# The first forward stage of a spectral mixing kernel: float32 products in place of a split pair

## The chip, the cores and the metric

The kernel runs on one core of a Trainium2 chip. The metric is device time in microseconds (us) for one run of the whole program. A core has engines that run side by side, each with its own queue of instructions taken strictly in the order in which the program lists them: PE (TensorE, matrix products; the loading of weights is shown apart as PEld), DVE (VectorE), ACT (ScalarE), POOL (GpSimd) and SP (SyncE, which here only starts transfers). POOL and ACT start a few transfers too. An engine waits for another by a semaphore.

## The reference

The input x has 2048 rows (s) and 512 columns (d). Two branches are computed from it and mixed by a gate of each row:

```
g = sigmoid(sum over d of x * gate_w)                 one number per row
a = irfft2( rfft2(x) * (w_r + i w_i) )                over rows and columns
b = gelu(x @ w1 + b1) @ w2 + b2                       w1 512 x 1792, w2 1792 x 512
out = g * a + (1 - g) * b
```

All of it is float32. rfft2 keeps 257 of the 512 column frequencies.

## The kernel before, in words

The Fourier transforms are done as matrix products with tables of cosines and sines, and the dense branch as plain matrix products. To reach float32 precision at the fast rate of PE, each operand is split into two parts of type float32r: a high part h, which ACT makes by a copy that rounds, and a low part l = value - h, which DVE makes by a subtraction. A product of two split operands is three PE products: h with h, h with l, l with h.

The rows are cut into 16 groups j of 128 rows. The forward stage is `forward(j)`, called once for each j in the order `NORD` (0, 4, 8, 12, 1, 5, ...):

- The columns of x are folded by symmetry. `eo` holds sums and differences of column blocks (L696, two DVE steps), `w` sums and differences of those (L699, two DVE steps). So `w` has four blocks of 128x128, by s (sum or difference) and c (cosine or sine).
- `w` is split into `eoh` (ACT, L704) and `eol` (DVE, L706). For j = 0 this is done in two halves, for the others in one step of 512 columns.
- The first stage multiplies them on PE with the column table `cf`, which was split when the program was built. `high` is four products, of 258 or 254 columns, of h with the table's high and low parts. `low` is four products of 130 columns, of l with the table's high part. They collect in the PSUM tile `pd`. The frequencies 0, 64, 128 and 192 have table entries that are exact without a low part, by scaling factors that a later table takes out again; this saves their low columns. The table is 2 x 128 x 576 elements.
- `pd` holds the high parts' sums and the low columns' sums in different places. ACT copies the first to the high part of `zb` (L745, two steps). DVE forms the low part of `zb` by a subtraction (L747, two steps), and adds the low columns' sums to it (L751, two steps). `zb` is the split input of the second stage. L754 reduces the gate's columns, which ride along in the table as extra columns written by L617 and L618 (high and low part), to the gate's logit.
- The second stage multiplies `zb` with the row table `tf` of this j (`py`, six products of 258 columns), and the results go to the big tile y.

Beside this the dense branch runs for four blocks c of 512 rows, in two halves of 7 of the 14 blocks f of w1 and w2: `ph` is x @ w1 for one block, gelu by ACT in PSUM (L1127), the split into `g` (L551, L552), and `po` is the product with w2. Each `ph` is 12 products of 512 columns, each `po` three for each f. The x of the dense branch is split into `mxh` and `mxl` (L642 to L647, L674 to L678), the weights into `wa..h`, `wa..l`, `wb..h`, `wb..l` (L1061 to L1069). Some weights' low parts are made by ACT (the negative of h) and a transfer of POOL that adds the original to it (L495).

After the forward stage follow, mostly on DVE, radix-4 steps and the filter, then for each c the inverse: `pz` (L987 and after) and `pa` products on PE, `od` (ACT), `u`, `v` and `w` (DVE, L1023 to L1033). For two of the four c the result is joined to the dense branch by an adding transfer of POOL (`w<-ba`) and stored (`out<-w`); for the last c the parts are joined on DVE (`o`, L1168 to L1209) and stored.

The order of all work is laid down when the program is built. Each step is entered in a graph with its engine, an assumed cost, the tiles that it reads and writes, and a rank. A list `RANKS` at the head of the file gives each step's rank; `schedule` then plays the graph through with the assumed costs, always taking the lowest rank that is ready, and the instructions are emitted in the order that comes out. All engines and the transfer queues are ordered in this way. PE's first instructions are 14 products of zeros (`none`) that warm it up.

Of the kernel before, what the change touches and what calls it, by code (L numbers as in the profile page):

```python
# [11 lines left out]
F32 = mybir.dt.float32  # L12
# [5 lines left out]
P = 128  # L18
# [3 lines left out]
HD = D // 2  # L22
# [4 lines left out]
TE, TW = 320, 576  # L27


EXACT = [0, 64, 128, 192]  # L30
NX = len(EXACT)
FORD = np.concatenate([np.arange(1, HD, 2), EXACT, [f for f in range(0, HD, 2) if f not in EXACT], [HD]])
# [23 lines left out]
def _tables():  # L56
# [3 lines left out]
    def cs(c, f):  # L60

        th = 2 * np.pi * np.asarray(f)[None, :] * d / D
        v = -np.sin(th) if c else np.cos(th)
        n = np.array([0.5 if g in (64, 192) else 1.0 for g in f])
        e = np.where(np.abs(v) > 0.6, np.where(n == 0.5, BIG, 1.0), SMALL) * np.sign(v)
        return np.where(np.isin(f, [*EXACT, HD])[None, :], e, v)

    BIG, SMALL = 2276 / 4096, 942.75 / 4096
    factor = np.ones(D)
    factor[128] = np.sqrt(2.0)  # L70
    factor[[64, 192]] = BIG * np.cos(np.pi / 8) + SMALL * np.sin(np.pi / 8)

    cf = np.zeros((2, P, TW), np.float32)
    even = FORD[P + NX:HD]
    for c in range(2):
        h, l = _split(cs(c, FORD[:P]))
        cf[c][:, :P], cf[c][:, P:2 * P] = l, h
        h, l = _split(cs(c, [*EXACT[c:], *even, *([HD] if c else [])]))
        cf[c][:, TE + 2:TE + 2 + P] = h
        cf[c][:, TE + 2 + P:TE + 2 + 2 * P - NX] = l[:, NX - c:P - c]  # L80
        assert not np.delete(l, np.arange(NX - c, P - c), 1).any()
# [8 lines left out]
    ]) / factor[f]  # L90
# [344 lines left out]
def tile_kernel(ctx: ExitStack, tc: tile.TileContext, xt, xc, w1, w2, b1, b2, x0g, wf, wrev, out, consts):  # L435
# [40 lines left out]

    def c_pe(n, k=1):
        return k * (n / 2400 + 0.0135) + 0.005

    def v(emit, n, reads, writes, rank=BULK, more=0.0):  # L480
        return add("vec", c_vec(n) + more, 0.12, emit, reads, writes, rank)

# [31 lines left out]

    gw, gs, gg = (one(n, [P, 2, 2], parts=2) for n in ("gw", "gs", "gg"))

    cft = buf("ctab", [P, 2, TW], F32R, "cf", parts=4)

    def cf_of(*cs):
        return [(cft, k) for c in cs for k in (c, 2 + c)]  # L520
# [802 lines left out]
```

## Time and profile before

| what | value |
| --- | --- |
| median of three runs | 372.4 us (372.05 to 372.67) |
| profiled execution, span from the first to the last instruction | 370.0 us |
| profiled execution's own time beside the span | not recorded apart; the runs' median is 2.4 us above the span |
| PE busy | 365.0 us, 1845 products |
| DVE busy | 337.1 us, 748 instructions |
| ACT busy | 224.2 us, 415 instructions |
| POOL busy | 34.0 us |
| moved by transfers | 61.20 MB, 165 GB/s on average |

The page gives busy time and share of the span for each engine, then the chain of work that ended last: followed backwards from the last instruction, at each step to what released it or to the instruction before it on its engine. A group's row gives line, engine, operation, output tile and input tiles, shapes, count, then busy time and the mean of one in ns, then the engine's idle time in front and what ended it. In a row of waits stand who waited, for whom, the total, the number of times and the longest. A row of a stage table has the stretch, its length, then busy us and count for PE, PEld, DVE, ACT and POOL, the granted clock of PE, the DMA share and GB/s; for one tile only the engines that touch it are listed. A line can be that of a helper: all products have L504, so they are told apart by their tiles. A PE product's listed length is longer than its distance to the next, because products are pipelined.

### The profile page before, as it was taken

How to read it: one execution, taken by the hardware profiler on the slowest of the kernel's cores; microseconds unless marked ns; L12 is line 12 of the kernel's file. 1: busy time of each engine (PE TensorE's matmuls, PEld its weight loads, DVE VectorE, ACT ScalarE, POOL GpSimd, SP SyncE). 2: the span in 40 equal slices, each digit the busy share in tenths (PEclk: the TensorE clock that was granted, in tenths of full speed). 3: DMA queues.
4: the chain of work that ended last, by engine and by line, in shares of the span. 5: the costliest groups of instructions: out<-in, count | busy, mean ns of one | idle time of the engine just before them, and what ended most of it. 6: DMA issues, size and time to landing. Idle time of an engine off the chain costs nothing.

```text
span 370.0 us, 5589 instructions
## 1 busy us (share of the span) xinstructions
PE 365.0 (99%) x1845; PEld 311.2 (84%) x1845; DVE 337.1 (91%) x748; ACT 224.2 (61%) x415; POOL 34.0 (9%) x54
## 2 busy tenths in 40 slices
PE   8999999999999999999999999999999999999996
PEld 7988888888888888888888888888888888888885
DVE  5999999999999999999989896789688999999993
ACT  5999676678724453555298349753955698653410
POOL 0133000000000000003033010000010000101110
PEclk9999999999999999999999999999999999999999
DMA  8999766195764582586769873216431053276456
GB/s 249 362 267 233 199 201 200 44 271 197 234 222 141 206 288 82 207 217 124 194 161 198 236 167 58 43 37 235 62 51 29 2 204 123 94 177 164 98 155 183
DMA packets 42053, 61.20 MB, mean 165 GB/s; under 512 B 4672, under 2 KB 22528, under 8 KB 41248
## 3 DMA queue, kind: packets, MB, share of 16 engines
q1 hardware_dynamic: 36120, 50.55, 41.5%
q0 software_dynamic: 5472, 9.96, 17.1%
q10 hardware_dynamic: 432, 0.33, 0.3%
q8 instruction: 14, 0.23, 0.2%
q14 instruction: 15, 0.12, 0.2%
HBM read 41.82 MB, written 16.92 MB: 159 GB/s over the span
## 4 chain that ended last, share of the span: by engine, by line
PE 97%; DMA 1%; SPq 1%; ACT 0%; issue 0%; DVE 0%; DVEq 0%
PE ph L504 41%; PE po L504 41%; PE pz L504 4%; PE pd L504 4%; PE py L504 3%; PE pa L504 3%; DMA war<-in_w 1%; PE po_23256r L504 0%; PE po_230r L504 0%; SPq L590 0%; SPq L1060 0%; ACT wa1h L1065 0%; SPq L594 0%; DVE o L1202 0%; PE pown L504 0%
## 5 line engine op out<-in xcount | busy, mean ns | idle before, releaser
L1127 ACT ACTIVATE ph<-ph,b1t 128x512 f32<-128x512 f32 x56 | 36.9, 658 | 51.0 <-PE ph L504 51.0
L963 ACT ACTIVATE sw<-y,al 64x512 f32<-64x512 f32 x32 | 22.9, 721 | 4.6 <-DVE y L826 2.1
L922 DVE TENSOR_TENSOR m<-y,wf 128x514 f32<-128x514 f32 x32 | 20.9, 688 | 0.1
L970 DVE SCALAR_TENSOR_TENSOR pq<-y,al,sw 128x256 f32<-128x256 f32 x32 | 14.6, 480 | 2.9 <-ACT sw L966 2.7
L504 PE MATMUL py<-zb,tf 128*128 128x258 f32 x96 | 16.7, 286 | 0.0
L504 PEld LDWEIGHTS py<-zb,tf 128*128 128x128 f32 x96 | 14.5, 190 | 1.2
L1177 ACT ACTIVATE o<-po,b2t 128x512 f32<-128x512 f32 x8 | 5.4, 688 | 16.6 <-PE po L504 16.5
L778 ACT ACTIVATE y<-pys 64x257 f32<-64x257 f32 x32 | 13.2, 417 | 3.3 <-DVE pys L775 2.6
L495 POOL DMA_DIRECT2D w<-ba x8 | 7.0, 899 | 77.8 <-ACT zb L990 46.2
L504 PEld LDWEIGHTS pa<-zb,ci 128*128 128x128 f32 x96 | 13.1, 190 | 1.0
L504 PE MATMUL pa<-zb,ci 128*128 128x256 f32 x96 | 13.4, 282 | 0.0
L699 DVE TENSOR_TENSOR w<-eo 128x256 f32<-128x256 f32 x32 | 13.0, 418 | 0.1
L696 DVE TENSOR_TENSOR eo<-xf 128x256 f32<-128x256 f32 x32 | 12.9, 416 | 0.0
L704 ACT ACTIVATE eoh<-w 128x512 fp32r<-128x512 f32 (+1 forms) x17 | 10.3, 606 | 4.3 <-DVE w L699 4.3
L495 POOL DMA_DIRECT2D bacc<-o x8 | 7.0, 873 | 63.6 <-ACT o L1181 50.5
L747 DVE TENSOR_TENSOR zb<-pd,zb 128x256 fp32r<-128x256 f32 x32 | 12.5, 417 | 0.3 <-ACT zb L745 0.3
L751 DVE TENSOR_TENSOR zb<-zb,pd 128x256 fp32r<-128x256 f32 (+1 forms) x32 | 12.3, 411 | 0.4
L745 ACT ACTIVATE zb<-pd 128x256 fp32r<-128x256 f32 x32 | 11.1, 384 | 1.6 <-PE pd L504 1.0
L495 POOL DMA_DIRECT2D wa7l<-in_w x1 | 0.9, 872 | 121.3 <-DVE g_1l L552 121.3
L706 DVE TENSOR_TENSOR eol<-w,eoh 128x512 fp32r<-128x512 f32 (+1 forms) x17 | 11.1, 652 | 0.3 <-PE pd L504 0.2
L991 DVE TENSOR_TENSOR zb<-pz,zb 128x512 fp32r<-128x512 f32 x16 | 10.9, 683 | 0.4 <-ACT zb L990 0.3
L990 ACT ACTIVATE zb<-pz 128x512 fp32r<-128x512 f32 x16 | 9.5, 594 | 2.7 <-PE pz L504 2.3
(596 smaller groups left out, 1297.5 us busy)
## 6 DMA issues: line engine op xcount, KB each, us to landing
wf<-in_wf SPq DMA_DIRECT2D x16, 257.0 KB, 3.5
bacc<-o SPq DMA_DIRECT2D x16, 256.0 KB, 2.8
xf<-in_xt SPq DMA_DIRECT2D x14, 256.0 KB, 4.2
wbr<-in_w SPq DMA_DIRECT2D x14, 256.0 KB, 3.6
war<-in_w SPq DMA_DIRECT2D x13, 256.0 KB, 3.9
xm<-in_xc SPq DMA_DIRECT2D x12, 256.0 KB, 4.0
tf<-tf SPq DMA_DIRECT2D x16, 192.0 KB, 3.4
bb<-bacc SPq DMA_DIRECT2D x8, 256.0 KB, 3.7
```

Of the source, the lines that this page charges most:

```text
L495: return add("pool", 2.3 * kb / 340, 3.4, lambda: nc.gpsimd.dma_start(dst(), src(), accum_op=ALU.add), reads, writes, rank)
L504: pe.matmul(ps, w, x, start=start, stop=stop)
L696: v(lambda s=s, op=op: vec.tensor_tensor(eo.ap()[:, s], x.ap()[:, 0:2], x.ap()[:, 2:4], op=op), 256, [x], [(eo, s)], feed)
L699: v(lambda s=s, op=op: vec.tensor_tensor(w.ap()[:, s], eo.ap()[:, :, 0], eo.ap()[:, :, 1], op=op), 256, [eo], [(w, s)], feed)
L706: v(lambda k=k: vec.tensor_tensor(l.ap()[:, k], w.ap()[:, k], h.ap()[:, k], op=ALU.subtract), 256 * len(ps), sub[0] + sub[1], sub[2], feed)
L747: v(lambda c=c: vec.tensor_tensor(segs(xl, c, 0, P + c), segs(ps, c, P, P + 4), segs(xh, c, 0, P + c), op=ALU.subtract), 256, [(ps, c), xh ...
L751: v(lambda o=o, i=i: vec.tensor_tensor(xl.ap()[:, :, o], xl.ap()[:, :, o], ps.ap()[:, :, i], op=ALU.add), 256, [ps], [xl], 0)
L778: a(lambda o=o, i=i: act.activation(Y[j].ap()[o:o + HP, 1], pys.ap()[i:i + HP, 1], AF.Copy), 257, [(pys, 1)], [(Y[j], 1 + k)], 0, more=0.1)
L922: v(lambda mk=mk, k=k, y=y, w=w: vec.tensor_tensor(mk.ap(), y.ap(), w.ap()[:, k:k + 1, :ND].to_broadcast([P, 2, ND]), op=ALU.mult), 514, [ ...
L963: a(lambda sw=sw, y=y, o=o, i=i: act.activation(sw.ap()[o:o + HP], y.ap()[i:i + HP, ::-1, :HD], AF.Copy, scale=al.ap()[i:i + HP, 0:1]), 51 ...
L970: v(lambda sw=sw, pq_=pq_, y=y, j=j, k=k, op=op: vec.scalar_tensor_tensor(pq_.ap()[:, k], y.ap()[:, k, :HD], al.ap()[:, 1 + j:2 + j], sw.a ...
L1127: a(lambda f=f, ps=ps: act.activation(ps.ap(), ps.ap(), AF.Gelu_apprx_tanh, bias=b1t.ap()[:, f:f + 1]), 600, [b1t], [ps], 0.9 if half else ...
```

## The change

The split of `w` goes. `w` itself, in float32, is multiplied with one float32 table. The four products of each j have 129 columns each; the two values of s no longer add up in the same columns of `pd` but stand in separate halves of it, since the fold by s already separates odd and even frequencies, so each product starts and stops its own sum. The table is 2 x 128 x 258 elements and has no low part; the exact frequencies with their factors are gone, in the table of the inverse as well, and the frequencies' order with them. The gate's columns need no low part. The two additions (L751) go. The tile `w` moves from the pool t2k (7 places) to the pool e2 (4 places), where `eoh` and `eol` were. The planner's assumed cost of the new products is written in `c_pe4`. All other functions are unchanged, but `RANKS` is a new list with a rank for each of the 1808 remaining steps, so the order of instructions on every engine is another one throughout.

```diff
-TE, TW = 320, 576
-EXACT = [0, 64, 128, 192]
-NX = len(EXACT)
-FORD = np.concatenate([np.arange(1, HD, 2), EXACT, [f for f in range(0, HD, 2) if f not in EXACT], [HD]])
+HW = P + 1
+FORD = np.concatenate([np.arange(1, HD, 2), np.arange(0, HD, 2), [HD]])
...
-    cf = np.zeros((2, P, TW), np.float32)
...
+    cf = np.zeros((2, P, 2 * HW), np.float32)
     for c in range(2):
...
+        cf[c][:, :P] = cs(c, FORD[:P])
+        cf[c][:, HW + 1:] = cs(c, FORD[P + c:HD + c])
...
-    ]) / factor[f]
+    ])
...
+    def c_pe4(n, k=1):
+        return k * (4 * n / 2400 + 0.027) + 0.005
...
-    cft = buf("ctab", [P, 2, TW], F32R, "cf", parts=4)
+    cft = buf("ctab", [P, 2, 2 * HW], F32, "cf", parts=4)
...
-        dma(lambda c=c: raw(cft.ap()[:, c], cf_d[c]), 288, [], [(cft, k) for k in (c, 2 + c)], 0.6)
+        dma(lambda c=c: sp.dma_start(cft.ap()[:, c], cf_d[c]), 129, [], [(cft, k) for k in (c, 2 + c)], 0.6)
...
-    gcol = [lambda k=k: cft.ap()[:, :, 2 * P + k:TE + k + 1:TE - 2 * P] for k in range(2)]
-    tiny(lambda: vec.tensor_copy(gcol[0](), gg.ap()), [gg], [(cft, 2), (cft, 3)])
-    tiny(lambda: vec.tensor_tensor(gcol[1](), gg.ap(), gcol[0](), op=ALU.subtract), [gg], [(cft, 2), (cft, 3)])
+    tiny(lambda: vec.tensor_copy(cft.ap()[:, :, P:P + 2], gg.ap()), [gg], [(cft, 2), (cft, 3)])
...
-        w = buf("t2k", [P, 2, 2, P], F32, f"w{j}", parts=2)
-        h, l = (buf("e2", [P, 2, 2, P], F32R, f"eo{k}{j}", parts=2) for k in "hl")
+        w = buf("e2", [P, 2, 2, P], F32, f"w{j}", parts=2)
...
-            a(lambda k=k: act.activation(h.ap()[:, k], w.ap()[:, k], AF.Copy), 256 * len(ps), sub[0], sub[1],
-              feed)
-            v(lambda k=k: vec.tensor_tensor(l.ap()[:, k], w.ap()[:, k], h.ap()[:, k], op=ALU.subtract),
-              256 * len(ps), sub[0] + sub[1], sub[2], feed)
...
-            m(high, NE, 4, [h, cft], [ps], 0)
-        m(low, 236, 4, [l, cft], [ps], 0)
+        def fold(s, cs):
+            for c in cs:
+                o = slice(HW, 2 * HW) if s == c else slice(0, HW)
+                mm(ps.ap()[:, c, o], w.ap()[:, s, c], cft.ap()[:, c, o], True, True)
+
+        for s in range(2):
+            if first:
+                for c in range(2):
+                    add("pe", c_pe4(HW), 0.25, lambda s=s, c=c: fold(s, (c,)), [(w, s), *cf_of(c)], [(ps, c)], 0)
+            else:
+                add("pe", c_pe4(HW, 2), 0.25, lambda s=s: fold(s, (0, 1)), [(w, s), cft], [ps], 0)
...
-        for o, i in ((slice(0, P), slice(0, P)), (slice(P + NX, 2 * P), slice(3 * P + NX, 4 * P))):
-            v(lambda o=o, i=i: vec.tensor_tensor(xl.ap()[:, :, o], xl.ap()[:, :, o], ps.ap()[:, :, i], op=ALU.add), 256, [ps],
-              [xl], 0)
...
 RANKS = """
...
```

More of the change, by code (lines that the diff above doesn't have):

```diff
@@ L62, in cs @@
         th = 2 * np.pi * np.asarray(f)[None, :] * d / D
[L63 to L71, printed above, removed]
-    cf = np.zeros((2, P, TW), np.float32)
-    even = FORD[P + NX:HD]
-    for c in range(2):
[L76 to L81, printed above, removed]
+        return -np.sin(th) if c else np.cos(th)
+    cf = np.zeros((2, P, 2 * HW), np.float32)
+    for c in range(2):
+        cf[c][:, :P] = cs(c, FORD[:P])
+        cf[c][:, HW + 1:] = cs(c, FORD[P + c:HD + c])
     f = FORD[:HD, None]
@@ L700, in forward @@
               [(w, s)], feed)
-        for k in (0, 1) if first else (slice(0, 2),):
-            ps = [k] if first else [0, 1]
-            sub = [[(b, p) for p in ps] for b in (w, h, l)]
-            a(lambda k=k: act.activation(h.ap()[:, k], w.ap()[:, k], AF.Copy), 256 * len(ps), sub[0], sub[1],
-              feed)
-            v(lambda k=k: vec.tensor_tensor(l.ap()[:, k], w.ap()[:, k], h.ap()[:, k], op=ALU.subtract),
-              256 * len(ps), sub[0] + sub[1], sub[2], feed)
         if j % 4 == 0:
@@ L714, in forward @@
         ps = buf("pf", [P, 2, 512], F32, f"pd{j}", parts=2, pool=pq)
-        odd, even = (slice(0, 2 * P + 2), slice(0, 2 * P + 2)), (slice(2 * P + 2, 4 * P), slice(TE, TE + 4 * P - 2 * P - 2))
-        odd_l, even_l = (slice(P, 2 * P + 2),) * 2, (slice(2 * P + 2, 3 * P + 4), slice(TE, TE + P + 2))
-        def high(ss=(0, 1), cs=(0, 1)):
-            for s in ss:
-                for c in cs:
-                    o, i = odd if s != c else even
-                    mm(ps.ap()[:, c, o], h.ap()[:, s, c], cft.ap()[:, c, i], s == 0, False)
-        def low():
-            for c in range(2):
-                for s in range(2):
-                    o, i = odd_l if s != c else even_l
-                    mm(ps.ap()[:, c, o], l.ap()[:, s, c], cft.ap()[:, c, i], False, s == 1)
-        if first:
-            for s in range(2):
+        def fold(s, cs):
[4 more added lines that the diff above has]
+            if first:
                 for c in range(2):
-                    m(lambda s=s, c=c: high((s,), (c,)), NE, 1, [(h, s), *cf_of(c)], [(ps, c)], 0)
-        else:
-            m(high, NE, 4, [h, cft], [ps], 0)
-        m(low, 236, 4, [l, cft], [ps], 0)
+                    add("pe", c_pe4(HW), 0.25, lambda s=s, c=c: fold(s, (c,)), [(w, s), *cf_of(c)], [(ps, c)], 0)
+            else:
+                add("pe", c_pe4(HW, 2), 0.25, lambda s=s: fold(s, (0, 1)), [(w, s), cft], [ps], 0)
         xh, xl = pair()
@@ L744, in forward @@
         for c in range(2):
-            a(lambda c=c: act.activation(segs(xh, c, 0, P + c), segs(ps, c, P, P + 4), AF.Copy), 256, [(ps, c)], [(xh, c)], 0)
+            a(lambda c=c: act.activation(segs(xh, c, 0, P + c), segs(ps, c, 0, P + 2), AF.Copy), 256, [(ps, c)], [(xh, c)], 0)
         for c in range(2):
-            v(lambda c=c: vec.tensor_tensor(segs(xl, c, 0, P + c), segs(ps, c, P, P + 4), segs(xh, c, 0, P + c), op=ALU.subtract),
+            v(lambda c=c: vec.tensor_tensor(segs(xl, c, 0, P + c), segs(ps, c, 0, P + 2), segs(xh, c, 0, P + c), op=ALU.subtract),
               256, [(ps, c), xh], [(xl, c)], 0)
-        for o, i in ((slice(0, P), slice(0, P)), (slice(P + NX, 2 * P), slice(3 * P + NX, 4 * P))):
-            v(lambda o=o, i=i: vec.tensor_tensor(xl.ap()[:, :, o], xl.ap()[:, :, o], ps.ap()[:, :, i], op=ALU.add), 256, [ps],
-              [xl], 0)
         n = j % 4 * 4 + j // 4
-        v(lambda: vec.tensor_reduce(logit.ap()[:, n:n + 1], ps.ap()[:, :, 2 * P:2 * P + 4], axis=mybir.AxisListType.XY, op=ALU.add),
+        v(lambda: vec.tensor_reduce(logit.ap()[:, n:n + 1], ps.ap()[:, :, P:P + 2], axis=mybir.AxisListType.XY, op=ALU.add),
           30, [ps, xl], [(logit, n)], 0)
```

147 rows, old and new, of the table RANKS are left out of this document.

## The prediction, made before the result was known

> **What bounds the kernel now.** I read the page's head and busy shares first, then the chain of waits by line, then who waited for whom on PE, then a table of busy time by stage. The first two say which engine sets the end.
>
> ```profile
> span 370.0 us, 5589 instructions
> ...
> PE 365.0 (99%) x1845; PEld 311.2 (84%) x1845; DVE 337.1 (91%) x748; ACT 224.2 (61%) x415; POOL 34.0 (9%) x54
> ...
> PE 97%; DMA 1%; SPq 1%; ACT 0%; issue 0%; DVE 0%; DVEq 0%
> ```
> ```profile
> by line: PE ph L504 41.4%; PE po L504 41.0%; PE pz L504 3.8%; PE pd L504 3.8%; PE py L504 3.2%; PE pa L504 3.1%; DMA war<-in_w 1.0%; PE po_23256r L504 0.3%; PE po_230r L504 0.3%; SPq L590 0.2%; SPq L1060 0.2%; ACT wa1h L1065 0.2%; SPq L594
> ```
> ```profile
> PE none L504 <- DVE own L796: 1.1, 1, 1.1
> PE ph L504 <- ACT wa1h L1065: 0.5, 1, 0.5
> ```
> ```profile
> 0.00:5.28 5.28, 4.23 (x14) 3.65 (x15) 1.65 (x7) 2.53 (x5) 0.65 (x16) 1.00 0.65 187
> 5.28:13.45 8.17, 7.65 (x63) 7.44 (x62) 7.66 (x23) 5.93 (x12) 0.00 (x0) 1.00 1.03 344
> 13.45:100.00 86.55, 86.55 (x484) 75.45 (x484) 82.57 (x218) 69.60 (x153) 7.19 (x8) 1.00 0.74 214
> ```
>
> 97% of the chain is PE, and PE waits for only one thing that is named after its warm-up: 0.5 us for a weight tile, near the start. The stage table (stretch, its length, busy PE, PEld, DVE, ACT, POOL with counts, granted clock, DMA share, GB/s) shows PE filled completely in the forward stage, 86.55 of 86.55 us, at full clock. DVE is busy there for 82.57 us, but the chain holds it at 0%. So a change is paid or earned on PE; time taken from DVE and ACT is worth only the gaps of PE that it closes.
>
> **What one PE instruction costs.** PE's own durations overlap, so I take the distance between starts. These rows are from the chain in order of time (start, length, what) and from the timeline.
>
> ```profile
> 12.66 0.95 PE pd L504 x8
> 19.62 0.72 PE py L504 x6
> 48.32 0.92 PE pd L504 x8
> 110.95 10.93 PE ph L504 x48
> ```
> ```profile
> 5.49 1.04 PE L504 MATMUL ph<-mxh,wa0h 128*128 128x128 f32 x8
> 6.37 0.69 PE L504 MATMUL ph<-mxl,wa0h 128*128 128x256 f32 x4
> 6.89 0.63 ACT L1065 ACTIVATE wa1h<-war 128x512 fp32r<-128x512 f32 x1 [1.49 <-DMA war<-in_w]
> 7.58 0.74 PE L504 MATMUL ph<-mxh,wa1h 128*128 128x256 f32 x4 [0.52 <-ACT wa1h L1065]
> ```
>
> 512 columns take 10.93/48 = 0.2277 us; the 258 columns of py take 0.72/6 = 0.120; 128 columns take (6.37 - 5.49)/8 = 0.110. Four times fewer columns than 512 save only half: below about 250 columns something that does not shrink with the columns, the change of weights most likely, paces PE. The old first stage sits on that floor: 3.8% of 370.0 us is 14.1 us for 128 instructions, 0.110 each (two sampled blocks of eight show 0.92 and 0.95).
>
> **The change, part by part.**
>
> *The products.* Out go eight products for each of the 16 j (four of 254 or 258 columns on the high half, four of 130 on the low half), 128 in all. In come four float32 products of 129 columns for each j, 64 in all. In the compiled program a float32 product is two weight loads and two multiplications: both programs hold 1845 of each. So PE's instruction count stays, and the whole question is the pace of the new 128. No row of this trace has a float32 product, so I bound it. Low end: each streams its 129 columns once and keeps the 0.110 of the 128-column row, 128 x 0.110 = 14.1, a difference of 0.0. High end: each streams 129 columns four times, or fails to hide its load, and costs the 512-column row, 128 x 0.2277 = 29.1, a difference of +15.0. I take each instruction as twice 129 = 258 columns, the py row: 128 x 0.120 = 15.4, hence **+1.3 us**. It is the row whose column count a product split over two instructions, high and low of both factors, would have.
>
> The Trainium skill (FP8 and Floating Point Precision, TensorE Precision Notes) says that true float32 takes four passes through the array, high and low of each factor against each other. An estimate from it is 4 x 129 = 516 columns a product, 0.229 at the 512-column row and 14.7 us for 64, +0.6 instead of +1.3. It speaks against the change, because the four products removed in each j for the low half are made again inside the array; no run here shows it yet.
>
> *VectorE and ScalarE.* These groups show what goes.
>
> ```profile
> L704 ACT ACTIVATE eoh<-w 128x512 fp32r<-128x512 f32 (+1 forms) x17 | 10.3, 606 | 4.3 <-DVE w L699 4.3
> L706 DVE TENSOR_TENSOR eol<-w,eoh 128x512 fp32r<-128x512 f32 (+1 forms) x17 | 11.1, 652 | 0.3 <-PE pd L504 0.2
> L747 DVE TENSOR_TENSOR zb<-pd,zb 128x256 fp32r<-128x256 f32 x32 | 12.5, 417 | 0.3 <-ACT zb L745 0.3
> L751 DVE TENSOR_TENSOR zb<-zb,pd 128x256 fp32r<-128x256 f32 (+1 forms) x32 | 12.3, 411 | 0.4
> ```
>
> The split into eoh and eol and the two additions behind the products (L751) go: 10.3 us of ACT, 11.1 + 12.3 = 23.4 us of DVE; the subtractions L747 stay. DVE falls from 82.6 to about 59 us in the forward stage, so it stops being nearly full there. None of this is on the chain. It can close only PE's gaps, and the size of those is this: in 13.45 to 100.00 there are 484 products, 122 of them pd (two begun earlier) and 96 py, by this pair of rows for the two tiles,
>
> ```profile
> 13.45:100.00 86.55, 17.09 (x122) 16.43 (x121) 26.54 (x80) 11.12 (x32) 1.00 0.74 214
> ```
> ```profile
> 13.45:100.00 86.55, 16.70 (x96) 14.51 (x96) 12.70 (x32) 6.14 (x16) 1.00 0.74 214
> ```
>
> which leaves 266 of 512 columns. 120 x 0.110 + 96 x 0.120 + 266 x 0.2277 = 13.2 + 11.5 + 60.6 = 85.3 us, so 1.3 us of the 86.55 are small gaps. The ends are all of it, -1.3, and as much again lost in the new order, +1.3. I take **-0.4**: the waits name no DVE step behind PE in this stage, so most of these gaps have another cause.
>
> *The table and the start.* The table shrinks from 2 x 288 to 2 x 129 KB and one tiny VectorE step on it (L618) goes. Both were ready before the first pd, and what is late next there is the fold: both kernels put the tables about tenth and twelfth in SP's queue. The new order matters more. SP's queue now has gw between the two halves of the first weight tile, and the second weight tile war (for wa1h) behind a 256 KB block of x instead of ahead of it. At the stage's 344 GB/s that block is 0.74 us, so wa1h and PE's wait for it move from 7.58 to about 8.3. ACT meanwhile makes the mxh that it made after wa1h before. In return PE has four products of wa0l, 4 x 0.120 = 0.48, placed in front of that wait. Net +0.26; I take **+0.2**. The stall now is 7.58 - (6.37 + 4 x 0.120) = 0.7 us, so the ends are -0.7 (all of it filled) and +0.7 (the late half tile delays wa0l too, and nothing fills the wait). Behind it the first float32 products wait for two fold steps of VectorE (L699, 0.42 each), now two j together; the steps that went from VectorE's queue pay for that.
>
> *The end.* The last pa block now stands nearer to the end.
>
> ```profile
> 351.70 1.12 PE L504 MATMUL pa<-zb,ci 128*128 128x256 f32 x8
> ...
> 360.22 0.89 POOL L495 DMA_DIRECT2D w<-ba  x1 [0.74 <-DVE o L1209]
> ...
> 363.30 1.06 SPq L1037 DMA_DIRECT2D out<-w  x2
> ...
> 366.29 0.28 PE L504 MATMUL po_23256r<-g_13h,wb13l 128*128 128x256 f32 x1
> 366.61 0.48 DVE L1202 TENSOR_TENSOR o<-y,po_23256r 128x128 f32<-128x128 f32 x2 [0.66 <-PE po_23256r L504]
> ```
>
> Before, pa's last eight start at 351.70 and PE's last product at 366.29. In the new order 45 products of 512 and 18 of 256 columns follow pa: 45 x 0.2277 + 18 x 0.119 = 12.4 us, about 1.5 less than now. The chain behind pa is the additions, POOL's accumulating DMA and out<-w at 363.30 to 364.36, issued 11.7 us behind pa's end (352.65). That still stands before the last o, at 12.4 + 0.8 behind pa. The DMA's landing is covered by a margin of about 1.5 us, and I cost it at **0**; with the cover gone it would cost up to that 1.5. POOL's order of accumulations stays but for two weight tiles.
>
> **Sum.** +1.3 - 0.4 + 0.2 + 0 = +1.1 us on the profiled 370.0, or 371.1. The median of the runs is 372.4, 2.4 above the profiled span; nothing in the change touches what lies around it, so 373.5.
>
> **The rivals.**
> - *No difference.* The new products keep the floor of 0.110: 0.0 - 0.4 + 0.2 gives 372.2. For it: the first stage ran at 0.110 with columns of 254 and 258 among them. Against: py, all 258, runs at 0.120.
> - *Faster.* VectorE and ScalarE, 34 us lighter, run ahead and every gap that they set closes, 1.3 in the forward stage and 0.7 at the start. With products half way between the two paces (0.115, +0.6) that is -1.4, or 371.0. It decides if the products cost under 2.0 - 0.7 = 1.3. Against: PE's named waits are for a DMA's tile, not for DVE.
> - *A late tile.* The new order of SP's queue brings one weight or x tile late by a landing, 3.9 us for war in this row, of which the queue ahead of PE covers about a third: +2.5 on the sum, 376.0.
>
> ```profile
> war<-in_w SPq DMA_DIRECT2D x13, 256.0 KB, 3.9
> ```
>
> - *The products are far dearer.* Four streams in each instruction, or loads that PE cannot run ahead of: the high end, +15.0 - 0.2, 387.2. Against it stands this row of loads of the same 128x128 and four-byte size, which run beside the products.
>
> ```profile
> L504 PEld LDWEIGHTS pd<-cf,eoh x64: 186/191/193, 12.5 to 90.7; 128*128 128x128 f32 x64
> ```
>
> The Trainium skill (TensorE: Matmul & The Clock Gate, Weight-path perf modes) says that the fast weight load is off for float32. If the old operands had it and the new ones lose it, this rival holds. Its section LDWEIGHTS gives 128 columns / 1.2 GHz = 107 ns for the ordinary load, and the 0.110 floor agrees, so the old operands seem not to have had it.
>
> **How the numbers follow.** Slower by the sum, 0.42 (its own range 373.2 to 375.5); no difference, 0.28; faster, 0.13; a late tile, 0.10; far dearer, 0.07. A difference under 0.2%, 0.74 us, is about what a measurement of this kernel cannot tell from none, so slower is 0.42 + 0.10 + 0.07 = 0.59, same 0.28, faster 0.13. The range 371.4 to 376.5 leaves out the dear products and about half of the faster case and of the late tile.
>
> **What would show it.** pd on the chain: 15.4 us (4.1%) if right, 14.1 for the floor, near 29 for the dear case; starts of pd 0.120 apart. DVE near 314 and ACT near 214 us busy, PE still over 98%. The first wa1h product at about 8.3. Between pd blocks, runs of 12 ph in 2.72 to 2.8 us. The prediction falls if PE shows a named wait of over 1 us behind the start, or if pd's pace is not near 0.120.

## The result, and the profile after

The changed kernel takes 374.2 us (median of 5 runs, 372.7 to 375.9) against 372.4 us before. The ratio of the two is 1.0056, with a 95% interval of 1.0039 to 1.0073: slower by 1.5 to 2.7 us. The prediction was 373.5 us, slower, within 371.4 to 376.5. The runs of the changed kernel also spread more: 3.2 us from the fastest to the slowest, where the five runs of before beside them spread over 0.6 us (in the later sessions, of 11 to 28 runs each, before spread over 1.0 to 2.2 us). The profiled execution is the fastest of the five, so it shows only a part of the loss.

From the page of the changed kernel, the span, the busy times and the chain by engine:

```profile
span 370.9 us, 5531 instructions
...
PE 365.3 (98%) x1845; PEld 310.8 (84%) x1845; DVE 316.0 (85%) x698; ACT 215.9 (58%) x398; POOL 34.1 (9%) x54
...
PE 91%; DMA 5%; ACT 1%; DVE 1%; SPq 0%; issue 0%; DVEq 0%
```

DVE fell by 21 us and ACT by 8, PE holds the same 1845 products, and the span is 0.9 us longer. The line to stop at is the last one. Before, 97% of the chain was PE; now it is 91%. The chain in order of time (start, length, what) shows where the other 9% lie:

```profile
4.99 4.84 DMA xm<-in_xc
...
10.23 4.31 DMA war<-in_w
...
14.93 5.79 DMA b2t<-in_b
20.82 0.42 DVE eo L672
...
29.04 0.70 DVE g_5l L531
29.78 2.33 PE po L483 x9
```

Up to 29.8 us the chain does not run on PE at all. It runs over transfers that land one after the other, then over DVE and ACT, which do their steps strictly in order. The last thing that PE had to wait for was a DVE step at 29.8 us; behind it PE is full to its last product. PE's number of products is the same and the new ones are not slower (below), so the loss of this execution is made in the first 30 us, but for 0.3 us at the end. The waits of PE behind its warm-up and the stages (stretch, length, busy PE, PEld, DVE, ACT, POOL, clock, DMA share, GB/s) name only a small part of it:

```profile
PE ph L483 <- ACT wa1h L1019: 0.5, 1, 0.5
PE ph L483 <- DVE mxl L624: 0.2, 1, 0.2
```
```profile
5.28:13.45 8.17, 7.46 (x59) 7.05 (x59) 8.00 (x23) 5.18 (x10) 0.00 (x0) 1.00 1.01 317
13.45:100.00 86.55, 86.44 (x486) 75.09 (x485) 71.83 (x186) 62.89 (x139) 7.17 (x8) 1.00 0.73 218
```

In the forward stage PE is as full as before, with DVE 11 us lighter. In 5.28 to 13.45 us PE has 59 products where it had 63, and 0.19 us less of busy time.

### The profile page after: what moved, and what is told of

Its sections match the earlier page's. It is cut to its first block, busy times and chain, and to the rows that moved or that the text cites. A ratio compares the mean times of both kernels' runs of the same rounds, so it can differ in the third digit from the quotient of the medians.

```text
span 370.9 us, 5531 instructions
## 1 busy us (share of the span) xinstructions
PE 365.3 (98%) x1845; PEld 310.8 (84%) x1845; DVE 316.0 (85%) x698; ACT 215.9 (58%) x398; POOL 34.1 (9%) x54
## 4 chain that ended last, share of the span: by engine, by line
PE 91%; DMA 5%; ACT 1%; DVE 1%; SPq 0%; issue 0%; DVEq 0%
PE po L483 41%; PE ph L483 37%; PE pz L483 4%; PE pa L483 3%; PE pd L483 3%; PE py L483 3%; DMA b2t<-in_b 2%; DMA xm<-in_xc 1%; DMA war<-in_w 1%; DMA xf<-in_x0g 1%; SPq L1018 0%; ACT ph L1081 0%; PE po_23256r L483 0%; PE po_230r L483 0%; DVE eo L672 0%; DVE g_5l L531 0%
## 5 line engine op out<-in xcount | busy, mean ns | idle before, releaser
L483 PE MATMUL pd<-cf,w 128*128 128x129 f32 x128 | 17.5, 274 | 0.0
L483 PEld LDWEIGHTS pd<-cf,w 128*128 128x128 f32 x128 | 16.4, 191 | 0.6
L483 PE MATMUL pa<-zb,ci 128*128 128x256 f32 x96 | 12.9, 283 | 0.0
L947 DVE TENSOR_TENSOR zb<-zb,pz 128x512 fp32r<-128x512 f32 x16 | 10.9, 685 | 0.3
L729 DVE TENSOR_TENSOR pys<-py,pys 128x257 f32<-128x257 f32 x16 | 6.7, 421 | 4.6 <-ACT pys L725 2.8
```

The source lines that it names most:

```text
L483: pe.matmul(ps, w, x, start=start, stop=stop)
```

## The experiments

They ask three questions: what the new arithmetic costs or gains by itself, what the new order does, and what in the order does it. One explanation of the order's cost is by transfers that land late in the first 35 us (where an expectation speaks of theory A, it is this one); its rivals are the order of PE's own work and single steps that block a queue. Unless it is said otherwise, the kernels compute the same as the changed one. Each ratio is against the kernel before, timed in the same session. The experiments set ranks, not orders: where a step is gone, added or made to wait, `schedule` plays the graph through again, and other steps can change places too. Where the traces show that this matters, it is said.

**The changed kernel again**, unedited, to know its spread.

> The changed kernel unedited, for a second trace. The recorded runs span 372.67 to 375.92 us, against 372.05 to 372.67 for the kernel before. Theory A (the new order leans on transfers that land late in the first 30 us): the profiled span moves between executions, 370.9 to 374, and the difference to the first trace lies in PE's gaps between 5 and 35 us. Theory B (the float32 products are what costs): spans stay within 0.5 us of each other in all but a rare run, and the pd blocks differ in no stretch from 0.11 us a start.

Measured: 374.8 us (374.0 to 375.4, 6 runs), ratio 1.0062 [1.005, 1.0074]. The loss repeats. This profiled execution, the slowest of the six, has a span of 373.6 us, 2.7 us more than the first, and the waits of PE name 2.0 us behind 20 us:

```profile
PE po L483 <- DMA wb13l<-in_w: 1.2, 1, 1.2
...
PE ph L483 <- DVE g_3l L531: 0.8, 1, 0.8
PE ph L483 <- ACT wa1h L1019: 0.3, 1, 0.3
```

There are two places: a DVE step at 23.8 us that had stood behind transfers, and at 215 us a weight tile that POOL's transfer brings. In the execution shown above POOL issues that transfer at 205.2 us and it lands in 4.8 us; here it is issued later, and it lands in 8.7. From POOL's timeline, first of the one above, then of this one, and the landing from this one's tile view:

```profile
205.17 0.86 POOL L474 DMA_DIRECT2D wb13l<-in_w  x1 [0.83 <-issue]
```
```profile
207.47 0.86 POOL L474 DMA_DIRECT2D wb13l<-in_w  x1 [0.73 <-ACT ph L1081]
```
```profile
DMA to landing us min/median/max: 8.7/8.7/8.7
```

Two transfers of x that SP issues at 209.1 and 209.5 us then run beside it. That they are what makes it slow is read from the times; it was not tried.

**New arithmetic in the old order.** `RANKS` is replaced: every step gets as its rank the place of the same step in the sequence of the kernel before.

```diff
 RANKS = """
-0 13 7 26 27 32 31 29 34 23 24 11 20 2 21 22 33 4 57 46 8 35 16 9 14 18 5 15 19 12 6 1 62 71 91 92 94 38 47 89 63 30
...
+0 15 16 25 27 29 31 34 36 37 41 8 21 1 20 24 28 22 58 45 7 12 17 10 2 18 9 13 19 5 4 14 50 59 69 68 88 44 56 60
...
```

> The new arithmetic with the ranks of the kernel before, so that every engine keeps its old order but for the steps that are gone. Theory A: the first stage on PE falls from 14.2 to 13.0 us and nothing else moves: 370.6 to 371.7 us, a ratio of 0.995 to 0.998, with a spread of the runs under 1 us. Theory B: 373.5 or more whatever the order, since products and table are those of the changed kernel.

Measured: 372.7 us (371.5 to 375.6, 12 runs), ratio 1.0018 [1.0, 1.0037], between the two. The spread is as wide as that of the changed kernel, and the profiled execution has one large wait of PE, with this piece on its chain:

```profile
PE py L485 <- ACT zb L704: 1.5, 1, 1.5
```
```profile
16.32 7.37 DMA war<-in_w
23.71 0.65 ACT wa6h L1021
```

A weight transfer took 7.4 us to land, ACT stood behind it, and `zb`, which is behind that in ACT's queue, came late for PE. So part of the loss is not in PE's order, and in this execution it hangs on a landing. The old order is not kept everywhere: by the traces 6 of PE's 1845 products and about 20 of SP's transfers stand at other places than in the kernel before.

**Old arithmetic in the new order.** The old kernel's steps follow the changed kernel's sequence; the steps that only it has stand behind the ones that they follow. Only `RANKS` differs from the kernel before.

```diff
 RANKS = """
-0 16 16 69 73 78 82 87 91 95 100 8 33 0 22 66 77 44 143 110 6 12 18 10 0 20 8 14 22 4 2 16 127 148 171 169 223 241
...
+0 150 160 250 270 290 310 340 360 380 420 80 210 10 220 230 280 110 580 490 50 140 190 70 120 170 20 130 180 100
...
```

> The old arithmetic (split fold, split table, two additions) with the ranks of the changed kernel. Theory A: the new order costs here as well, and more, since VectorE has 23 us more to do: 374.5 to 377 us, with runs 2 to 3 us apart. Theory B: the order is neutral, 372.0 to 373.0.

Measured: 389.0 us, ratio 1.0454 [1.0439, 1.0469]. The largest waits of PE, and its stage from 50 to 100 us:

```profile
PE ph L515 <- DVE g_2l L563: 4.6, 1, 4.6
PE py L515 <- ACT pys L782: 2.8, 2, 1.5
```
```profile
50.00:100.00 50.00, 42.67 (x233) 36.88 (x233) 45.20 (x114) 31.22 (x73) 0.00 (x0) 0.93 0.37 111
```

PE loses 7.3 us there to DVE and ACT, and its granted clock falls to 0.93. The new order counts on the DVE steps that are gone. An order is thus only as good as the arithmetic that it was made for, and this run alone can't tell what the order costs the new arithmetic.

**Every float32 product twice**, into the same place (the output is the same; the work is double).

```diff
-                mm(ps.ap()[:, c, o], w.ap()[:, s, c], cft.ap()[:, c, o], True, True)
+                for _ in range(2):
+                    mm(ps.ap()[:, c, o], w.ap()[:, s, c], cft.ap()[:, c, o], True, True)
```

> The changed kernel with each of the 64 float32 products issued twice into the same place, so 128 more PE instructions on the path and nothing else. With the pace seen in the trace, 0.102 to 0.111 us each, the time rises by 13.0 to 14.2 us to 387 to 388.5. With the pace of the prediction, 0.120, it rises by 15.4. If it rises by less than 11, PE has gaps that the extra products fill.

Measured: 386.0 us (385.9 to 386.4), ratio 1.0371 [1.0358, 1.0384]: 11.2 to 11.8 us above the changed kernel's two medians for 128 more PE instructions, 0.087 to 0.092 each in time, less than was expected. Their pace is on the chain:

```profile
13.36 3.57 PE pd L483 x32
```

3.57/32 = 0.112 us from start to start. Against the first profiled execution of the changed kernel the span grew by 384.7 - 370.9 = 13.8 us, 0.108 for each. So against that execution PE pays for the products almost in full. The lower figure in the medians is most likely due to the waits that the changed kernel has in other executions: the runs with doubled products spread over 0.5 us only, and 97% of the chain is PE.

**Four small transfers late.** b2t, rev, al and the first ti (2, 32, 9 and 64 KB) are issued by SP between 6 and 15 us in the changed kernel, and needed much later (b2t at 99.7 us). Here they, and the three tiny DVE steps on b2t and rev, wait until about 45 us.

```diff
     def load_small():
         dma(lambda: sp.dma_start(b1t.ap(), b1), 7, [], [b1t], 0.45)
-        dma(lambda: sp.dma_start(b2t.ap(), b2), 2, [], [b2t])
+
+    def load_rest():
+        then = [(logit, 4)]
+        dma(lambda: sp.dma_start(b2t.ap(), b2), 2, then, [b2t])
...
-            dma(lambda w=w, j=j: sp.dma_start(w.ap(), ti_d[j]), 64, [], [w], 3)
+            dma(lambda w=w, j=j: sp.dma_start(w.ap(), ti_d[j]), 64, [(logit, 4)] if j == 1 else [], [w], 3)
...
+        if n == 4:
+            load_rest()
```

> The changed kernel with four transfers that nothing needs before 48 us (b2t, rev, al and the first ti, 107 KB in small rows) and the three tiny VectorE steps behind them moved out of the first 30 us to about 45 us. Theory A (SP's queue and the transfers of the first 35 us bound the changed kernel): four issues of 0.45 us and 107 KB come out of the crowded stretch, so the weight and x tiles land 0.5 to 1.5 us earlier: 372.8 to 373.8 us against 374.2 to 374.8, and runs closer together. Rival B2 (PE's lost time comes from the order on PE, ACT and VectorE alone, transfers do not matter): 374.2 to 374.8 as before.

Measured: 372.57 us (372.2 to 374.3, 12 runs), ratio 1.0007 [0.9997, 1.0017]. Almost the whole loss against before is gone, and PE has no named wait behind its warm-up. The profiled execution does not show what was gained: its span, 370.9 us, is that of the changed kernel's first one, and its chain leaves DVE and ACT at 29.6 us still. Only the share of transfers in it is smaller:

```profile
PE 91%; DVE 2%; DMA 2%; ACT 2%; SPq 1%; issue 1%; DVEq 0%; ACTq 0%
```

So it is the slow executions that are gone (eleven of the twelve runs lie within 1.1 us). The edit also does more than it says: with the four places of SP free, the planner put other transfers first. Rows of SP's timeline, first of the changed kernel, then of this one:

```profile
7.90 0.33 SPq L1018 DMA_DIRECT2D war<-in_w  x1
...
9.16 0.33 SPq L650 DMA_DIRECT2D xm<-in_xc  x1
```
```profile
6.87 0.43 SPq L670 DMA_DIRECT2D xm<-in_xc  x1
7.58 0.33 SPq L1038 DMA_DIRECT2D war<-in_w  x1
```

The second block of x (xm) is now issued ahead of war and 2.3 us earlier. By the traces seven of SP's other transfers and five ACT steps stand elsewhere (the copy mxh eight places earlier), while PE's order is the same but for three products. This change of order is a rival to the transfers themselves.

**The start as before**: SP's first eight transfers in the old sequence, and ACT's wa1h ahead of the copy of an x block (mxh) that stands before it in the changed kernel. Again only `RANKS` differs, in ten steps' ranks relative to each other.

```diff
 RANKS = """
-0 13 7 26 27 32 31 29 34 23 24 11 20 2 21 22 33 4 57 46 8 35 16 9 14 18 5 15 19 12 6 1 62 71 91 92 94 38 47 89 63 30
...
+0 150 160 250 270 290 310 340 360 380 420 80 200 10 210 240 280 220 580 490 50 140 190 70 120 170 20 130 180 100
...
```

> The changed kernel with the first eight transfers of SP in the order of the kernel before (gw behind the x halves, the weight tile of wa1h ahead of x of group 8) and wa1h ahead of that x's copy on ACT. If the start is what the new order costs: the first wa1h product returns from 8.1 to 8.6 us towards 7.6, pd starts at 12.5, and the time falls by 0.3 to 0.7 us. If what happens from 15 to 35 us hides it, 0.0 to 0.2.

Measured: 373.25 us (372.6 to 376.2, 12 runs), ratio 1.0027 [1.0013, 1.0042]. It recovers 0.3% of the changed kernel's 0.56 to 0.62%, but not the spread of 3.6 us.

**Old order and the small transfers late**, with the new arithmetic: `RANKS` by the sequence of before, and `load_small` and ti edited as in the run of the small transfers.

```diff
 RANKS = """
-0 13 7 26 27 32 31 29 34 23 24 11 20 2 21 22 33 4 57 46 8 35 16 9 14 18 5 15 19 12 6 1 62 71 91 92 94 38 47 89 63 30
...
+0 150 160 250 270 290 310 340 360 370 410 80 210 10 200 240 280 220 580 450 70 120 170 100 20 180 90 130 190 50
...
```

> The new arithmetic in the old order (372.74 us median) with the same four small transfers moved to about 45 us. Theory A: the landing that ACT waited for near 24 us comes earlier, the wait of py closes (1.5 us in that trace), and the first stage's saving shows: 371.0 to 372.0, faster than the kernel before. Rival B2: 372.5 to 373.0.

Measured: **371.0 us (370.9 to 371.4, 5 runs), ratio 0.996 [0.9948, 0.9972]**. It beats both kernels, by 1.6 us and 3.3 us, and its runs spread over 0.5 us. Page and waits of PE:

```profile
span 369.2 us, 5544 instructions
...
PE 99%; DVE 0%; DVEq 0%; issue 0%
```
```profile
PE none L501 <- DVE own L771: 1.1, 1, 1.1
```

99% of the chain is PE, from its warm-up on.

**One more transfer**, 256 KB of x into a tile that nobody reads, issued behind the two halves of the table.

```diff
+    more = one("more", [P, NQ, P])
+    dma(lambda: sp.dma_start(more.ap(), xt[0]), 256, [], [more], 0.6)
```

> The changed kernel with one more transfer of 256 KB that nobody reads, right behind the table's two, the opposite of the previous edit. At the 340 to 370 GB/s of that stretch it is 0.7 us of transfer time and 0.45 us of SP's queue. Theory A: 0.5 to 1.5 us slower than the changed kernel, 375 to 376 us. Rival B2: no difference, under 0.3 us.

Measured: 374.3 us (373.6 to 374.6, 4 runs), ratio 1.0044 [1.0032, 1.0057]: no slower than the changed kernel. All other transfers keep their order here, and those behind the new one are issued later, xm at 10.6 us instead of 9.2:

```profile
10.58 0.33 SPq L669 DMA_DIRECT2D xm<-in_xc  x1
```

So the plain explanation by the volume that is moved falls, and the run speaks against a later issue of these tiles alone as the cause: 256 KB more and 1.4 us later cost nothing that can be seen, while the edit that took 107 KB away brought 0.5%.

**The kernel before with the small transfers late**, the control for the 371.0 us: old arithmetic, old order, and the same edit of `load_small` and ti.

> The kernel before, arithmetic and order as they were, with the same four small transfers (b2t, rev, al, the first ti) and the three DVE steps on them moved to about 45 us, as in the run with the old order and the new arithmetic that came out at 370.96 us. PE of the kernel before has no wait between 8 and 370 us, and b2t lands there in 3.8 us at 8.3 us, before the queues fill. If the 370.96 us came from the arithmetic (pd 14.22 to 12.29 us on PE), with the transfers only removing waits that the new arithmetic had opened, this stays at 372.2 to 372.6 us. If it came from the transfers, whatever the arithmetic, this falls by the same 1.4 us, to 370.8 to 371.2 us. Between the two, both have a share.

Measured: 372.54 us (372.0 to 373.5, 12 runs), ratio 1.0008 [0.9998, 1.0017]. No gain. So the 371.0 us need the new arithmetic; late transfers alone bring nothing. PE's order in the kernel of 371.0 us is that of the kernel before, product for product, and in this control it differs by 12 products. SP, DVE and ACT are planned anew with the lighter steps: about 20, 85 and 30 of their steps stand elsewhere, so what is called the arithmetic's here includes that. The tile view of `pd` (durations in ns, first and last start) shows where PE gains. First this control, then the kernel of 371.0 us:

```profile
L499 PE MATMUL pd<-cf,eoh x64: 277/283/334, 12.9 to 91.4; 128*128 128x258 f32 x32, 128*128 128x254 f32 x32
...
L499 PE MATMUL pd<-cf,eol x64: 219/274/278, 13.3 to 92.1; 128*128 128x130 f32 x64
```
```profile
L501 PE MATMUL pd<-cf,w x128: 271/274/276, 12.4 to 90.5; 128*128 128x129 f32 x128
```

From the first pd to the last it is 92.1 - 12.9 = 79.2 us against 90.5 - 12.4 = 78.1: 1.1 us less with the same 448 products. The first pd is another 0.5 us earlier. (In the profiled execution of the kernel before the two starts are 12.5 and 91.4, 78.9 us apart.)

**Only the DVE steps late**: the transfers of the changed kernel stay, and the three DVE steps on b2t and rev wait until 45 us.

```diff
     def load_small():
...
-        add("vec", 0.1, 0.1, lambda: vec.tensor_scalar(nb2.ap(), b2t.ap(), -1.0, None, op0=ALU.mult), [b2t], [nb2], 3)
...
+    def use_rest():
+        then = [(logit, 4)]
+        add("vec", 0.1, 0.1, lambda: vec.tensor_scalar(nb2.ap(), b2t.ap(), -1.0, None, op0=ALU.mult), [b2t, *then], [nb2], 3)
```

> The changed kernel with only the three small DVE steps on b2t and rev (nb2, and two on rev) moved to about 45 us; all transfers stay where they are. If the 1.9 us that came back when the small transfers went late were DVE standing in its queue behind b2t (issued at 14.9 us, landed at 20.7), this gives the same: 372.3 to 373.0 us. If they came from the transfers' own places in SP's queue and in the transfer engines, this stays at 373.8 to 374.8 us.

Measured: 374.3 us (373.0 to 378.2, 11 runs), ratio 1.0057 [1.0032, 1.0081]. Nothing comes back. The chain of the changed kernel names b2t and the DVE step behind it, but that step is not the cause. With it gone the chain still holds 10% of transfers, and PE waits for the same `g_3l` and, at 215 us, for the same tile of POOL (this execution, 376.6 us, is one of the slowest of the eleven). Chain by engine, and waits of PE:

```profile
PE 74%; DMA 10%; DVE 9%; ACT 3%; issue 2%; POOL 1%; SPq 0%; DVEq 0%; POOLq 0%; ACTq 0%
```
```profile
PE po L500 <- DMA wb13l<-in_w: 2.4, 1, 2.4
...
PE ph L500 <- DVE g_3l L548: 0.6, 1, 0.6
```

**b2t early**: only rev, al, ti and the steps on rev are late (the edit is against the kernel with all four late).

```diff
     def load_small():
         dma(lambda: sp.dma_start(b1t.ap(), b1), 7, [], [b1t], 0.45)
+        dma(lambda: sp.dma_start(b2t.ap(), b2), 2, [], [b2t])
+        add("vec", 0.1, 0.1, lambda: vec.tensor_scalar(nb2.ap(), b2t.ap(), -1.0, None, op0=ALU.mult), [b2t], [nb2], 3)
```

> The changed kernel with rev, al, the first ti and the two DVE steps on rev moved to about 45 us, while b2t and the DVE step on it stay in their early places. If b2t and the DVE step behind it are what costs, this stays at 373.8 to 374.8 us. If it is the larger small transfers (rev 32 KB, al 9 KB, ti 64 KB, in short rows) that hold the transfer engines at 10 to 25 us, this gives 372.3 to 373.0 us.

Measured: 373.2 us (372.0 to 377.0, 12 runs), ratio 1.003 [1.0008, 1.0052]. The value lies between the two that were expected, with an interval that comes within 0.04% of either (1.0007 and 1.0056): inconclusive.

**Four tiny transfers in their places**: the kernel with the small transfers late, and four transfers of 2 KB into unread tiles at the four places of SP's queue that had come free.

```diff
         dma(lambda: sp.dma_start(b1t.ap(), b1), 7, [], [b1t], 0.45)
+        for k in range(4):
+            un = one(f"un{k}", [P, NQ])
+            dma(lambda un=un: sp.dma_start(un.ap(), b2), 2, [], [un])
```

> The changed kernel with its four small transfers late (the 372.57 us run), and four transfers of 2 KB each, into tiles that nobody reads, put on SP's queue at the four places that were left. SP then issues as much between 6 and 16 us as in the changed kernel, but 8 KB instead of 107 KB, and DVE has no step on any of it. Each issue holds SP for 0.43 to 0.48 us, so the transfers behind come 0.5 us later per place, up to 1.9 us. If the places in SP's queue (or the number of transfers) are what costs, this is at 373.8 to 374.8 us like the changed kernel. If it is the bytes and rows of rev, al and ti, it stays at 372.3 to 372.9 us.

Measured: 373.5 us (373.0 to 374.9, 6 runs), ratio 1.0043 [1.0028, 1.0059]. Against the kernel with the small transfers late that is 0.36% (1.0043 - 1.0007), two thirds of the changed kernel's loss, though the four transfers move 8 KB that nobody reads. What they carry is thus not what counts for most of it. But the four transfers are not all that came back. With the places taken, the planner makes the changed kernel's order of the large transfers again; xm stands behind war once more:

```profile
7.99 0.33 SPq L1041 DMA_DIRECT2D war<-in_w  x1
...
9.31 0.33 SPq L673 DMA_DIRECT2D xm<-in_xc  x1
```

Seven large transfers and four ACT steps differ from the kernel with the four late, and only one of each from the changed kernel. So the 0.36% belong to the four places together with the order that goes with them. Which of the two costs it, the transfers or the order, is not shown; a kernel with the large transfers' order held fixed and the four left out was not run. If it is the transfers, a candidate is that each issue holds SP, for 0.33 to 0.43 us in this run (the row of b2t in the changed kernel's tile view: shortest, median and longest in ns, first and last start):

```profile
L599 SPq DMA_DIRECT2D b2t<-in_b x1: 430/430/430, 14.9 to 14.9; - x1
```

Another is their 128 short rows; the two aren't told apart here. The Trainium skill (DMA: Bandwidth & Descriptors, Queues, rings and completion order) says that each transfer engine takes SP's descriptors in the order of its ring. The changed kernel's chain agrees: b2t's 2 KB, issued behind large tiles, took 5.79 us to land. The rest up to the changed kernel (0.13 to 0.19%) can't be told from the spread.

Put together from the ratios, with 0.1% as 0.37 us (the intervals of the single ratios are 0.1 to 0.2% to each side):

| step | from, to | ratio | us |
| --- | --- | --- | --- |
| new arithmetic, old order, small transfers late | 1.0008 to 0.9960 | -0.48% | -1.8 |
| new order, small transfers late | 0.9960 to 1.0007 | +0.47% | +1.8 |
| four tiny transfers in SP's queue, and the order of the large ones that comes with them | 1.0007 to 1.0043 | +0.36% | +1.3 |
| what these transfers carry (not resolved) | 1.0043 to 1.0056 or 1.0062 | +0.13 to 0.19% | +0.5 to 0.7 |

The split holds for this path. With the small transfers at their early places the new arithmetic in the old order costs 0.18% (its interval begins at zero) instead of gaining 0.48%, and the new order 0.38 to 0.44% on top. Why the early transfers cost the new arithmetic 0.58% in the old order and the old arithmetic nothing stays open; one trace names a landing of 7.4 us.

## Why the prediction was right or wrong

The time came out right (slower, 0.7 us off the median), but by terms that are wrong on both sides and nearly cancel.

**The products: the step that failed.** It took each new instruction as 258 columns, the py row at 0.120 us, for +1.3. The runs show less, and a gain. These rows of PE's timeline (start, length) show a block of eight and what follows, first before, then after:

```profile
48.16 0.56 PE L504 MATMUL pd<-cf,eol 128*128 128x130 f32 x4
48.55 0.69 PE L504 MATMUL pd<-cf,eoh 128*128 128x254 f32 x4
49.08 0.53 PE L504 MATMUL py<-zb,tf 128*128 128x258 f32 x3
```
```profile
57.32 1.05 PE L483 MATMUL pd<-cf,w 128*128 128x129 f32 x8
58.12 0.85 PE L483 MATMUL py<-zb,tf 128*128 128x258 f32 x5
58.82 0.40 PE L483 MATMUL po<-g_6h,wb6h 128*128 128x512 f32 x1
```

49.08 - 48.16 = 0.92 us from the block's first start to py before, 58.12 - 57.32 = 0.80 after. Some of that comes back at once: five py take 58.82 - 58.12 = 0.70 us, not 5 x 0.120 = 0.60. The pace inside long blocks is 0.112 (the run with doubled products). So the new pair sits on the 0.110 floor of the "no difference" rival, and the old block was not there: half of its instructions, those of 254 and 258 columns, are py rows at 0.120, of which the prediction itself had the row (from start to start in the trace of before, medians by pair of shapes: 0.118 to 0.121, and 0.110 between those of 130 columns). 64 x (0.120 - 0.112) = 0.5 us, less 64 x 0.002 = 0.1 that the other half gives back, of the 1.1 that the stage lost against the control (0.8 against the profiled execution of before); the rest is at the blocks' ends and in gaps. The low end of 0.0 was therefore no bound. The prediction's own test, a pace "not near 0.120", tells against it, and so does its other one, a named wait of over 1 us behind the start: the second execution of the same kernel has one (wb13l, 1.2 us).

The estimate from the Trainium skill (FP8 and Floating Point Precision, TensorE Precision Notes), four passes or 0.229 a product, is met by 2 x 0.112 = 0.224; but two loads at the floor give 0.22 as well, so these runs can't tell four passes from two. The rival of lost weight loads falls: the loads' median is the same before and after (191 and 192 ns), so the old operands had no faster load to lose. The Trainium skill (TensorE: Matmul & The Clock Gate, Weight-path perf modes) says that the fast weight load is off for float32; that it was off for float32r as well is read from this row and the one in the prediction:

```profile
L483 PEld LDWEIGHTS pd<-cf,w x128: 187/192/192, 12.9 to 91.3; 128*128 128x128 f32 x128
```

**DVE and ACT, -0.4: not seen apart.** Their busy times came as said (316.0 and 215.9 us against 314 and 214). But in the forward stage DVE fell to 71.83 us and not to about 59: other steps of DVE run there in the place of those that are gone (with PE's old order, in the kernel of 371.0 us, it is 74.70). PE is no fuller in it than before, 86.44 of 86.55 us. What was closed is part of the 1.1 us above and can't be separated from the pace.

**The start, +0.2 with ends of ±0.7: the mechanism right, the size too small.** wa1h did move, further than said, and the four wa0l products were put in front of it as read from the order:

```profile
7.34 0.74 PE L483 MATMUL ph<-mxh,wa0l 128*128 128x256 f32 x4
8.59 0.73 PE L483 MATMUL ph<-mxh,wa1h 128*128 128x256 f32 x4 [0.50 <-ACT wa1h L1019]
```

8.59 us instead of the 8.3 that was forecast. With the old start the ratio fell from 1.0056 (1.0062) to 1.0027, so the start is worth about 1.1 to 1.3 us (by the intervals 0.3 to 2.0). The step reckoned with one 256 KB block ahead of one tile. It left out that everything behind in SP's queue moves too, and that DVE and ACT are on the chain up to 29.8 us; that these two make up the difference is argued, not shown. (The tables stand 12th and 14th in SP's queue after the change, not tenth and twelfth; the sum did not use it.)

**The end, 0: +0.3.** From the last product's start to the end of the span it is now 370.9 - 366.89 = 4.0 us. Before, the last product started at 366.29 and the span ended at 370.0: 3.7. The last row of PE after:

```profile
366.89 0.28 PE L483 MATMUL po_23256r<-g_13h,wb13l 128*128 128x256 f32 x1
```

**The late tile, 0.10 at 376.0: it is there, in some executions.** wb13l cost PE 1.2 us in one profiled execution and 2.4 in another, nothing in the one shown first. It is POOL's tile, not SP's.

**The base.** The prediction set the time 2.4 us above the span. The runs since show 1.8 (372.67 against 370.9 in the profiled execution after, 370.96 against 369.2 in the kernel of 371.0 us). So the profiled execution of before took near 371.8 us, 0.6 less than the median. The forecast doesn't suffer, since its sum is a difference that was added to the median, 372.4 + 1.1; but the 2.4 us are not time that lies around the span, as it was read.

In sum, products and relief together were put at +0.9 and measured -1.8 with the small transfers late; the order, with the small transfers in SP's queue, was put at +0.2 and measured +3.6 to +3.8 by the ratios. By the other path, with the transfers early, it is +0.7 and +1.4 to +1.6. That the total came near the forecast is luck.

## What to carry to other kernels

Where PE is full, a change that swaps products is read from the pace of starts of each shape that goes, not from the mean of the group: a mean of 0.110 hid that half of the old instructions ran at 0.120. Look at the share of PE in the chain and at the time from which on the chain is PE. The kernels here with 97% or more of PE spread over 0.5 to 2.2 us, those with 69 to 92% over 1.0 to 5.2; but 91% is the share of the kernel that lost almost nothing (small transfers late) as well as of the changed one, so it is a warning and not a measure. When an order is made anew, try to move early transfers that are needed late out of the busy stretch, however small, and then compare the orders that the planner made of it: one edit can move more than it names. And time the new arithmetic in the old order, because the two effects can hide each other.

## What was not expected of the hardware

- A float32 product of 129 columns runs as two instructions 0.112 us apart, hardly more than a 128-column float32r product (0.110), with weight loads of 192 ns against 191 for float32r.
- Four transfers of 2 KB, together with the order of the large ones that came with them, cost 0.9 us by the medians and 1.3 us by the ratios, and one of 256 KB nothing to be seen, while the transfer engines were full (share 1.03 between 5 and 25 us in the changed kernel).
- The landing of a 256 KB tile is not a constant: 3.9 us in the median of war before, but 7.4 us in the first 25 us of one run, and 4.8 or 8.7 us for the same wb13l in two executions of one program.
